# Moving the additions to the softmax sums from GpSimd to VectorE, and one weight step ahead of the copy of h, in a fused attention and feed-forward kernel

## The chip, the core and the metric

The kernel runs on one core of a Trainium2 chip. The metric is the device time of one execution in microseconds (us). The kernel before takes 947.29 us, the median of three runs (945.96 to 948.33).

A core has five engines that run side by side, each working through its own queue of instructions in the order in which the program issued them. TensorE (PE in the profile; its weight loads are PEld) multiplies matrices into eight PSUM banks. VectorE (DVE), ScalarE (ACT) and GpSimd (POOL) do arithmetic on tiles. SyncE (SP) issues the transfers here. Where one engine needs another's result it waits on a semaphore, and everything behind the waiting instruction in the same queue waits with it.

## The reference, cut to what matters

```
scores = q @ k^T / 8, masked to a window of 32 keys (half of the heads: 32 keys at distance 4)
attn   = exp(scores - max);  attn = attn / (sum(attn) + 1e-09)
x      = (attn @ v), heads put side by side        # 4608 tokens x 512
h      = x @ w_in                                  # 512 -> 2048
sp     = max(h, 0) + log1p(exp(-abs(h)))
out    = (h * erf(sp)) @ w_out                     # 2048 -> 512
```

All data is float32. The `+ 1e-09` under the division is the addition that the change moves.

## The kernel before, in words

**Attention.** The work is cut into 72 units (u or n) of four blocks of 64 queries for two heads. A unit passes through `scores` (TensorE, into the banks `sp`), `mask_max` (VectorE: masked scores into `prob`, their maxima into `nmax`), `exponents` (ScalarE: four exponentials in place, each with its row sums into `ssum`; then GpSimd adds 1e-9 to the sums, L207), `normalize` (VectorE: reciprocals `rinv` of the sums, L211; then GpSimd multiplies `prob` by them, L212), `transposes` (TensorE, L217), `turned` (a copy to `pT`, L220), `values` (TensorE, L233), `rows_hi` (ScalarE, L274) and `rows_lo` (VectorE, L279), which write the rounded value and the remainder of the rows x. Values follow scores three visits later (LAG = 3).

**Feed-forward.** It is made in 72 steps t of 512 tokens by 256 hidden columns, each of two half steps; x = 2t + j counts half steps. One half step runs `mm1` (12 matmuls into the single bank `h`, L454), `take` (VectorE copies `h` to `hc`, L462, which frees the bank), and, two steps later, `mm2` (L495). Between them stand `argument` (ScalarE: Sigmoid L466 and Ln L467), `table` (ScalarE: Erf, L470) and `gate` (VectorE, L477, L480, L481). Functions in different tables cost a table load on ScalarE.

**Weights.** The float64 weights are split on the chip into a rounded part and a remainder. One step is `prep_act` (ScalarE: a cast L377 and a rebased copy L382) and `prep_dve` (VectorE: a subtraction L391 and three bit operations L395 to L397, after which SyncE loads the next piece, L366).

**Order.** The order on every engine is the order in which the code issues (`manual_schedule`). The first 14 units (FIRST = 14) go through `first_visit`, before any feed-forward. Then the half steps begin: x = 0 to 3 belong to steps 0 and 1, in which there is no `mm2` yet. Half step x (up to 6) scores unit 14 + x and finishes unit 11 + x. In x = 0 to 3, TensorE gets the transposes of the finished unit first, then `mm1`, then `values` and `scores`. The weight step stands behind `take`, and is left out at x = 2 and 3 (`pause`), so that of these four half steps only x = 0 and x = 1 have one. `exponents` of what was scored at x come at x + 1 for x = 0, and at even half steps otherwise; `normalize` of a unit comes at the earliest one half step after its `exponents`, behind whatever `exponents` that half step issues.

Of the kernel before, what the change touches and what calls it, by code (L numbers as in the profile page):

```python
# [15 lines left out]
ALU = mybir.AluOpType  # L16
# [46 lines left out]
FIRST = NBLK + LAG + 2  # L63
# [5 lines left out]
SAVED = 2 * (HALF + 1) + 1  # L69
# [16 lines left out]
def ends(t):  # L86

    return t + 1 == NT or STEPS[t][2] != STEPS[t + 1][2]
# [24 lines left out]
def attn_moe_kernel(ctx: ExitStack, tc: tile.TileContext, qk, v, masks, eye, w_in, w_out, out):  # L113
    nc = tc.nc
# [50 lines left out]
    def load_qk(u):  # L165
        if u < NU:
            n = QW + key_start(u, PER - 1) + KEYS
            nc.sync.dma_start(out=qkz[u % 2][:, 0:n], in_=qk[u, :, 0:n])
# [5 lines left out]
    probs, maxes, sums, x_rows = {}, {}, {}, {}  # L174
# [24 lines left out]
    def exponents(u):  # L199
        nmax = maxes.pop(u)  # L200
        sums[u] = small.tile([P, PER], F32, name="ssum", bufs=LAG + 1)
        for j in range(PER):
            nc.scalar.activation(  # L203
                out=probs[u][:, j, :], in_=probs[u][:, j, :], func=AF.Exp,
                scale=-1.0, bias=nmax[:, j:j + 1], accum_out=sums[u][:, j:j + 1],
            )
        nc.gpsimd.tensor_scalar(sums[u], sums[u], 1.0e-9, None, op0=ALU.add)  # L207

    def normalize(u):
        rinv = small.tile([P, PER], F32, name="rinv")  # L210
        nc.vector.reciprocal(out=rinv, in_=sums.pop(u))  # L211
        nc.gpsimd.tensor_tensor(probs[u], probs[u], rinv.broadcast_to([P, PER, KEYS]), op=ALU.mult)  # L212

    def transposes(u):
        pr = probs.pop(u)
        for j in range(PER):
            nc.tensor.transpose(out=turn_place(u)[0:KEYS, j * P:(j + 1) * P], in_=pr[:, j, :], identity=ident)  # L217

    def turned(u, copy):
        copy(out=pz[u in second][0:KEYS].rearrange("p j q -> p (j q)"), in_=turn_place(u)[0:KEYS])  # L220

    def turn(units):
        for u in units:
            transposes(u)
        for u in units:
            turned(u, nc.vector.tensor_copy)
# [75 lines left out]
    def has(u):  # L302
        return 0 <= u < NU
# [46 lines left out]
    def soon(load, *args):  # L350
        if held[0]:
            behind.append((load, args))
        else:
            load(*args)

    def hold(on):
        held[0] = on
        while behind and not on:
            load, args = behind.pop(0)
            load(*args)  # L360
# [10 lines left out]
    def prep_act():  # L371


        calls[0] += 1
        if made:
            w, hi, lo = made.popleft()
            nc.scalar.copy(out=hi, in_=w)  # L377
            rest.append((calls[0], w, hi, lo))
        if staged:
            i, d, hi, lo = staged.popleft()  # L380
            w = io.tile([P, TOK], F32, name="w", bufs=4)
            nc.scalar.activation(out=w, in_=d[:, :, 1].bitcast(F32), func=AF.Abs, scale=REBASE)  # L382
            begun.append((calls[0], i, d, hi, lo, w))

    def prep_dve(keep=None):

        if rest and rest[0][0] < calls[0]:
            _, w, hi, lo = rest.popleft()  # L390
            nc.vector.tensor_tensor(lo, w, hi.bitcast(F32), op=ALU.subtract)  # L391
        if begun and begun[0][0] < calls[0]:
            _, i, d, hi, lo, w = begun.popleft()
            t = w.bitcast(I32)
            nc.vector.tensor_scalar(t, t, 3, None, op0=ALU.logical_shift_left)  # L395
            nc.vector.scalar_tensor_tensor(t, d[:, :, 1], -0x80000000, t, op0=ALU.bitwise_and, op1=ALU.bitwise_or)  # L396
            nc.vector.scalar_tensor_tensor(t, d[:, :, 0], 29, t, op0=ALU.logical_shift_right, op1=ALU.bitwise_or)  # L397
            made.append((w, hi, lo))
            if i != keep:
                soon(load_w, i)  # L400
# [82 lines left out]
    def mm2(t, j):  # L483
        ghi, glo = gs[t][j]
        _, ftp, run = STEPS[t]
        ft = ftp * PAIR + j
        first, last = ftp == RUNS[run][1] and j == 0, ends(t) and j == PAIR - 1
        parts = ((ghi, wout_hi), (ghi, wout_lo)), ((glo, wout_hi),)

        if last:  # L490
            parts = (sum(parts, ()),)
        for part in parts:
            for tt in range(TOK // P):
                for g, w in part:
                    nc.tensor.matmul(acc[tt], g[:, tt * P:(tt + 1) * P], w[:, ft, :],  # L495
                                     start=(first and w is wout_hi and g is ghi),
                                     stop=(last and g is glo))
        if j == PAIR - 1:
            del gs[t]
# [37 lines left out]
    with tc.manual_schedule():  # L537
        load_qk(0)
        nc.sync.dma_start(out=cst, in_=masks)
        for t in vz:  # L540
            nc.gpsimd.memset(t[KEYS:P], 0.0)
        nc.gpsimd.memset(pz[0][KEYS:P], 0.0)
        load_qk(1)
        nc.sync.dma_start(out=ident, in_=eye)
        for n in range(FIRST):
            if n < 3:
                load_w(n)
            first_visit(n)
            if 1 <= n <= EARLY:
                prep_dve()  # L550
        normalize(FIRST - 2)
        rows_lo(FIRST - 1 - LAG)

        plan = visits()


        pause = 2, 3, 2 * (USED[SPC - 1] + 1) - 2
        due = {n - LAG: x for x, ns in plan.items() for n in ns}
        todo, scaled, fresh = [], [FIRST - 1], []
        for x in range(2 * (NT + 2)):  # L560
            t, j = divmod(x, 2)
            ns = plan.get(x, [])
            scored, ready = [n for n in ns if has(n)], [n - LAG for n in ns]
            second.update(ready[1:])

            if t < 2:
                turn(ready)
            if t < NT:
                after = STEPS[t + 1][0] if ends(t) and t + 1 < NT else None
                if x == 2 * HALF - 4:  # L570
                    load_x(1, range(twice))
                elif after and after > 1 and j == 0:
                    load_x(after, range(twice))
                if x in (2 * HALF - 2, SAVED):
                    hold(True)
                mm1(t, j)
                if x == 0:
                    for a in stores:
                        store_x(*a)
                if after is not None and j == PAIR - 1:  # L580
                    load_x(after, range(twice, CC))
                    hold(False)
                take(t, j)

            if x == 1 or j == 0 and x:
                for u in todo:
                    exponents(u)
                fresh, todo = todo, []
            if j == 1 and 1 <= t <= NT:
                table(t - 1)  # L590
            if t < 2:
                attend(ready, scored)
            if t >= 2:
                turn(ready)

            while scaled:
                normalize(scaled.pop(0))
            scaled, fresh = fresh, []
            if j == 1 and 1 <= t <= NT:
                gate(t - 1, 0)  # L600
            if j == 0 and 2 <= t:
                gate(t - 2, 1)
            if j == 1 and t < NT:
                argument(t)
            if x not in pause:
                prep_act()
                prep_dve(keep=2 if SAVED - 4 < x <= SAVED else None)
            if t >= 2:
                mm2(t - 2, j)
                if x == SAVED:  # L610
                    save()
                    hold(False)
                    load_w(2)
                elif ends(t - 2):
                    if j == 1:
                        store(STEPS[t - 2][0])
                    elif STEPS[t - 2][2] == 2:
                        fetch()
            if t >= 2:
                attend(ready, scored)  # L620
            for n in ns:
                soon(load_qk, n + 2)
                soon(load_v, n - 1)
            for n in scored:
                mask_max(n)
                todo.append(n)
            for u in [u for u in scaled if due[u] == x + 1]:
                scaled.remove(u)
                normalize(u)
            for m in ready:  # L630
                rows_lo(m)
            if x == SAVED + 2:
                nc.gpsimd.memset(pz[1][KEYS:P], 0.0)
        assert not todo and not prep and not staged and not begun and not made and not rest
# [84 lines left out]
```

## Time and profile before

| | |
|---|---|
| median of 3 runs | 947.29 us |
| the profiled execution | 947.37 us, of which the span from first to last instruction is 945.6 us |
| mean granted TensorE clock | 0.996 of full speed |
| busy: DVE, ACT, POOL | 581.6, 643.3, 109.3 us |
| first matmul into h (x = 0) | 51.12 us after the span's start |
| first matmul of x = 1, 2, 3, 4 | 55.54, 61.18, 71.52, 77.17 us |

Times in the rows below count from the start of the span. A row of the timeline reads: start, duration, engine, line of the code, operation, output from input; in brackets the idle time of the engine just before it and what ended that.

### The profile page before, as it was taken

How to read it: one execution, taken by the hardware profiler on the slowest of the kernel's cores; microseconds unless marked ns; L12 is line 12 of the kernel's file. 1: busy time of each engine (PE TensorE's matmuls, PEld its weight loads, DVE VectorE, ACT ScalarE, POOL GpSimd, SP SyncE). 2: the span in 40 equal slices, each digit the busy share in tenths (PEclk: the TensorE clock that was granted, in tenths of full speed). 3: DMA queues.
4: the chain of work that ended last, by engine and by line, in shares of the span. 5: the costliest groups of instructions: out<-in, count | busy, mean ns of one | idle time of the engine just before them, and what ended most of it. 6: DMA issues, size and time to landing. Idle time of an engine off the chain costs nothing.

```text
span 945.6 us, 15964 instructions
## 1 busy us (share of the span) xinstructions
PE 917.9 (97%) x6048; PEld 749.5 (79%) x6048; DVE 581.6 (62%) x1509; ACT 643.3 (68%) x1204; POOL 109.3 (12%) x154
## 2 busy tenths in 40 slices
PE   5879999999999999999999999999999999999998
PEld 4657887888888887888888888888888888888886
DVE  6967988986665654666566555655665444434434
ACT  7878978785856865777577656866566556445553
POOL 2312210011111210121111111111111000000000
PEclk9999999999999999999999999999999999999999
DMA  8774443431632242313232152314220302011001
GB/s 284 263 240 139 175 172 138 145 122 51 211 133 68 67 150 73 111 67 111 87 111 67 67 164 103 120 45 140 91 87 35 107 10 87 1 45 44 1 1 45
DMA packets 51500, 98.73 MB, mean 104 GB/s; under 512 B 7136, under 2 KB 20192, under 8 KB 51424
## 3 DMA queue, kind: packets, MB, share of 16 engines
q1 hardware_dynamic: 51136, 97.19, 30.7%
q8 instruction: 48, 0.79, 0.3%
q10 hardware_dynamic: 288, 0.52, 0.1%
q14 instruction: 28, 0.23, 0.1%
HBM read 69.52 MB, written 27.26 MB: 102 GB/s over the span
## 4 chain that ended last, share of the span: by engine, by line
PE 89%; DVE 5%; DMA 2%; ACT 2%; issue 1%; POOL 0%; SPq 0%; POOLq 0%; DVEq 0%
PE h L454 40%; PE acc L495 39%; PE tx L233 3%; PE sp L184 3%; PE sp L217 3%; DMA x<-xT 1%; DVE w L396 1%; DVE w L397 1%; DMA qk<-in_qk_dram 1%; DVE win_lo L391 1%; DVE prob L193 1%; DVE w L395 0%; DMA dbl<-in_w_in_dram 0%; PE acc L217 0%; DVE x L279 0%
## 5 line engine op out<-in xcount | busy, mean ns | idle before, releaser
L462 DVE COPY hc<-h 128x512 f32<-128x512 f32 x144 | 99.4, 691 | 281.7 <-PE h L454 281.3
L454 PE MATMUL h<-x,win_hi 128*128 128x512 f32 x832 | 260.1, 394 | 1.4 <-DMA x<-xT 1.3
L495 PE MATMUL acc<-wout_hi,ghi 128*128 128x512 f32 x576 | 227.5, 395 | 0.2 <-DVE ghi L480 0.2
L495 PE MATMUL acc<-wout_lo,ghi 128*128 128x512 f32 x576 | 224.4, 390 | 0.0
L466 ACT ACTIVATE s<-hc 128x1024 f32<-128x1024 f32 x72 | 76.4, 1061 | 182.5 <-DVE hc L462 182.5
L454 PEld LDWEIGHTS h<-x,win_hi 128*128 128x128 f32 x832 | 155.2, 189 | 36.2 <-issue 2.1
L454 PE MATMUL h<-x,win_lo 128*128 128x512 f32 x416 | 162.6, 391 | 0.0
L495 PE MATMUL acc<-wout_hi,glo 128*128 128x512 f32 x576 | 158.8, 389 | 0.0
L495 PEld LDWEIGHTS acc<-wout_hi,ghi 128*128 128x128 f32 x576 | 108.2, 188 | 22.6 <-DVE ghi L480 0.6
L495 PEld LDWEIGHTS acc<-wout_hi,glo 128*128 128x128 f32 x576 | 108.1, 188 | 22.6
L495 PEld LDWEIGHTS acc<-wout_lo,ghi 128*128 128x128 f32 x576 | 108.3, 188 | 21.4
L481 DVE TENSOR_TENSOR glo<-s,ghi 128x512 fp32r<-128x512 f32 x144 | 107.8, 749 | 5.2
L203 ACT ACTIVATE prob<-prob,nmax 128x96 f32<-128x96 f32 x288 | 104.0, 363 | 5.4 <-DVE nmax L193 5.0
L212 POOL TENSOR_TENSOR prob<-prob,rinv 128x384 f32<-128x384 f32 x72 | 86.2, 1208 | 113.4 <-DVE rinv L211 104.4
L477 DVE TENSOR_TENSOR s<-hc,s 128x1024 f32<-128x1024 f32 x72 | 89.3, 1240 | 6.8 <-ACT s L470 6.6
L467 ACT ACT_TABLE_LOAD x72 | 92.4, 1283 | 1.3
L470 ACT ACT_TABLE_LOAD x72 | 92.4, 1283 | 1.3
L454 PEld LDWEIGHTS h<-x,win_lo 128*128 128x128 f32 x416 | 78.5, 189 | 16.9
L193 DVE CUSTOM_DVE_ANT_0 prob<-sp,cst 128x96 f32<-128x96 f32 x288 | 54.7, 252 | 49.4 <-PE sp L184 49.3
L454 PE MATMUL h<-dbl,win_hi 128*128 128x512 f32 x256 | 80.6, 396 | 0.0
L207 POOL TENSOR_SCALAR ssum<-ssum 128x4 f32<-128x4 f32 x72 | 20.3, 282 | 496.2 <-ACT prob L203 485.2
L274 ACT CAST rows<-tx 128x64 fp32r<-128x64 f32 (+5 forms) x116 | 26.2, 357 | 75.2 <-PE tx L233 75.2
(59 smaller groups left out, 1016.8 us busy)
## 6 DMA issues: line engine op xcount, KB each, us to landing
xT<-rows SPq DMA_DIRECT2D x26, 576.0 KB, 4.8
v<-in_v_dram SPq DMA_DIRECT2D x72, 192.0 KB, 4.0
qk<-in_qk_dram SPq DMA_DIRECT2D x48, 272.0 KB, 3.9
dbl<-in_w_in_dram SPq DMA_DIRECT2D x16, 512.0 KB, 4.0
dbl<-in_w_out_dram SPq DMA_DIRECT2D x16, 512.0 KB, 3.3
qk<-in_qk_dram SPq DMA_DIRECT2D x24, 288.0 KB, 4.1
out_dram<-w SPq DMA_DIRECT2D x26, 256.0 KB, 2.4
x<-xT SPq DMA_DIRECT2D x8, 320.0 KB, 5.7
```

The lines of the kernel that those rows point to most:

```text
L184: nc.tensor.matmul(sps[h][r:r + BLK, i, j // 2, :], qkz[i][hs, j * BLK:(j + 1) * BLK], qkz[i][hs, at:at + KEYS], start=True, stop=True)
L193: nc.vector.tensor_tensor_reduce(out=pr[:, 2 * h + p, :], in0=sps[h][:, u % 2, p, :], in1=mask[PAIRS.index((kind(n), kind(n + 1)))], scale ...
L203: nc.scalar.activation(out=probs[u][:, j, :], in_=probs[u][:, j, :], func=AF.Exp, scale=-1.0, bias=nmax[:, j:j + 1], accum_out=sums[u][:, ...
L212: nc.gpsimd.tensor_tensor(probs[u], probs[u], rinv.broadcast_to([P, PER, KEYS]), op=ALU.mult)
L454: nc.tensor.matmul(h, w[:, cc, ft * P:(ft + 1) * P], x[cc], start=(k == 0 and i == 0), stop=(k == CC - 1 and i == 2))
L462: nc.vector.tensor_copy(out=hs[t][:, j], in_=h)
L466: nc.scalar.activation(out=ls[t], in_=hs[t], func=AF.Sigmoid, scale=-1.0)
L467: nc.scalar.activation(out=ls[t], in_=ls[t], func=AF.Ln, bias=TINY)
L470: nc.scalar.activation(out=ls[t], in_=ls[t], func=AF.Erf, scale=-1.0)
L477: nc.vector.tensor_tensor(out=e, in0=hc, in1=e, op=ALU.mult)
L481: nc.vector.tensor_tensor(out=glo, in0=e[:, j], in1=ghi.bitcast(F32), op=ALU.subtract)
L495: nc.tensor.matmul(acc[tt], g[:, tt * P:(tt + 1) * P], w[:, ft, :], start=(first and w is wout_hi and g is ghi), stop=(last and g is glo))
```

## The change

It does two things. In `exponents` and `normalize`, units from 14 on have 1e-9 added to their sums by VectorE, as the instruction right in front of the reciprocals, instead of by GpSimd behind the exponentials; units 0 to 13 stay as they were. In the half steps of steps 0 and 1, the weight step is issued behind the copies of `turn` and in front of `mm1` and the copy of `h`, instead of behind them; from step 2 on it stays where it was.

```
     def exponents(u):
...
-        nc.gpsimd.tensor_scalar(sums[u], sums[u], 1.0e-9, None, op0=ALU.add)
+        if u < FIRST:
+            nc.gpsimd.tensor_scalar(sums[u], sums[u], 1.0e-9, None, op0=ALU.add)

     def normalize(u):
         rinv = small.tile([P, PER], F32, name="rinv")
+
+        if u >= FIRST:
+            nc.vector.tensor_scalar(sums[u], sums[u], 1.0e-9, None, op0=ALU.add)
         nc.vector.reciprocal(out=rinv, in_=sums.pop(u))
...
         pause = 2, 3, 2 * (USED[SPC - 1] + 1) - 2
+
+        def weights(x):
+            if x not in pause:
+                prep_act()
+                prep_dve(keep=2 if SAVED - 4 < x <= SAVED else None)
+
...
             if t < 2:
                 turn(ready)
+                weights(x)
...
             if j == 1 and t < NT:
                 argument(t)
-            if x not in pause:
-                prep_act()
-                prep_dve(keep=2 if SAVED - 4 < x <= SAVED else None)
             if t >= 2:
+                weights(x)
                 mm2(t - 2, j)
```

The changed file has other line numbers: what was L211, L212, L391, L395, L462 is L215, L216, L395, L399, L466 there.

VectorE at x = 0 before: the copy of unit 11's transposes, the copy of h, the reciprocals of unit 13, then the weights.

```order
L220 COPY pT_88<-acc_93 96x512
L462 COPY hc<-h 128x512
L211 RECIPROCAL rinv<-ssum 128x4
L391 TENSOR_TENSOR wout_lo<-w,wout_hi 128x512
L395 TENSOR_SCALAR w<-w 128x512
L396 SCALAR_TENSOR_TENSOR w<-dbl_552,w 128x512
L397 SCALAR_TENSOR_TENSOR w<-dbl_552,w 128x512
```

And the same place of the changed kernel:

```order
L224 COPY pT_88<-acc_93 96x512
L395 TENSOR_TENSOR wout_lo<-w,wout_hi 128x512
L399 TENSOR_SCALAR w<-w 128x512
L400 SCALAR_TENSOR_TENSOR w<-dbl_552,w 128x512
L401 SCALAR_TENSOR_TENSOR w<-dbl_552,w 128x512
L466 COPY hc<-h 128x512
L215 RECIPROCAL rinv<-ssum 128x4
```

The four weight instructions went in front of the copy of h; x = 1 has the same move. At x = 2, and wherever reciprocals of later units stand, one small `TENSOR_SCALAR ssum<-ssum 128x4` now stands right in front of them.

GpSimd before, from the last unit of the first visits on; the pairs are units 12 and 13, then the sums of 14 and 15, then their products, and so on.

```order
L207 TENSOR_SCALAR ssum<-ssum 128x4
L212 TENSOR_TENSOR prob<-prob,rinv 128x384 x2
L207 TENSOR_SCALAR ssum<-ssum 128x4 x2
L212 TENSOR_TENSOR prob<-prob,rinv 128x384 x2
L207 TENSOR_SCALAR ssum<-ssum 128x4 x2
```

And in the changed kernel:

```order
L208 TENSOR_SCALAR ssum<-ssum 128x4
L216 TENSOR_TENSOR prob<-prob,rinv 128x384 x6
L437 CAST x_99<-x_99 128x2x64
L437 CAST x_100<-x_100 128x2x64
L216 TENSOR_TENSOR prob<-prob,rinv 128x384 x5
```

The product of unit 14 no longer stands behind the sums of unit 15; nothing but products, two casts and one memset is left on GpSimd from here to the end.

ScalarE at x = 0 and x = 1 before: the rows of unit 11, the exponentials of 14, the rows of 12, Sigmoid and Ln of step 0, the weight step of x = 1, and then the exponentials of 15 and the rows of 13 (that of x = 0 stands between the first two).

```order
L274 CAST rows<-acc_94 128x256
L466 ACT_TABLE_LOAD
L466 ACTIVATE s<-hc 128x1024
L467 ACT_TABLE_LOAD
L467 ACTIVATE s<-s 128x1024
L377 CAST wout_hi<-w 128x512
L382 ACTIVATE w<-dbl_657 128x512
L203 ACT_TABLE_LOAD
```

And in the changed kernel:

```order
L381 CAST wout_hi<-w 128x512
L386 ACTIVATE w<-dbl_657 128x512
L203 ACTIVATE prob,ssum<-prob,nmax 128x96 x4
L278 CAST rows<-acc_94 128x256
L470 ACT_TABLE_LOAD
L470 ACTIVATE s<-hc 128x1024
L471 ACT_TABLE_LOAD
L471 ACTIVATE s<-s 128x1024
L203 ACT_TABLE_LOAD
```

The weight step of x = 1 went from behind the Ln to in front of unit 14's exponentials. On SyncE the load that each moved weight step issues moves with it: that of x = 0 now stands in front of the four stores of x to `xT` that were ahead of it. The order on TensorE is the same.

## The prediction

> **What bounds the kernel now.** I first read the page's busy times, to see whether any engine has no room.
>
> ```profile
> PE 917.9 (97%) x6048; PEld 749.5 (79%) x6048; DVE 581.6 (62%) x1509; ACT 643.3 (68%) x1204; POOL 109.3 (12%) x154
> ```
>
> TensorE is busy for 917.9 of 945.6 us, so a change elsewhere can pay only by closing some of the other 28 us. The view of waits says where they are; this is TensorE from 50 to 82 us, and then from 82 us to the end (total, times, longest).
>
> ```profile
> PE acc L217 <- POOL prob L212: 5.6, 2, 5.3
> PE acc L233 <- DVE pT L220: 1.1, 1, 1.1
> ```
>
> ```profile
> PE h L454 <- DMA x<-xT: 1.3, 3, 0.5
> PE tx L233 <- DVE pT L220: 1.0, 1, 1.0
> PE acc L495 <- DVE ghi L480: 0.2, 1, 0.2
> ```
>
> From 82 us on TensorE waits 2.5 us in all; between 50 and 82 us, the half steps that the change touches, it waits 6.7 us, and 5.3 us of it at one place. The chain that ended last, around that place, names the culprit (start, duration, what).
>
> ```profile
> 51.36 2.76 PE h L454 x12
> ...
> 65.53 0.51 ACT wout_hi L377
> 66.03 0.56 ACT w L382
> ...
> 69.61 0.22 POOL ssum L207
> ...
> 69.90 0.84 POOL prob L212
> ...
> 71.87 4.26 PE h L454 x12
> ```
>
> At x = 3 TensorE wants unit 14's transposes and waits for GpSimd's product of unit 14. Why was that late? The timelines of GpSimd and of VectorE tell.
>
> ```profile
> 60.12 0.22 POOL L207 TENSOR_SCALAR ssum<-ssum 128x4 f32<-128x4 f32 x1 [3.93 <-ACT prob L203]
> 69.60 0.22 POOL L207 TENSOR_SCALAR ssum<-ssum 128x4 f32<-128x4 f32 x1 [9.26 <-ACT rows L274]
> ```
>
> ```profile
> 64.83 0.17 DVE L211 RECIPROCAL rinv<-ssum 128x4 f32<-128x4 f32 x1
> ```
>
> Unit 14's sums were ready at 60.34 us and its reciprocals at 65.0, but the product stands in GpSimd's queue behind the addition to unit 15's sums, and that waited 9.26 us for ScalarE's exponentials. The product lost 4.9 us (69.90 against 65.0) to a queue, not to data. It cost more than the wait: the clock fell too (windows of 5 us; the column behind the five engines is the granted clock).
>
> ```profile
> 60.00:65.00 5.00, 4.86 (x66) 3.76 (x61) 4.93 (x17) 4.56 (x6) 0.22 (x1) 1.00 0.96 320
> 65.00:70.00 5.00, 0.50 (x18) 0.31 (x16) 0.89 (x9) 4.95 (x15) 0.32 (x2) 0.81 0.69 236
> 70.00:75.00 5.00, 4.22 (x12) 3.50 (x13) 1.18 (x3) 2.23 (x2) 0.73 (x1) 0.50 0.29 118
> ```
>
> At clock 0.50 the 12 matmuls of x = 3 took 4.26 us; those of x = 0, at full clock, took 2.76.
>
> **The change part by part.** I follow x = 0 to 5 with both edits in.
>
> *Weights ahead of the copy, x = 0.* VectorE's rows at x = 0 and 1:
>
> ```profile
> 54.15 0.69 DVE L462 COPY hc<-h 128x512 f32<-128x512 f32 x1 [2.06 <-PE h L454]
> ...
> 54.84 0.66 DVE L391 TENSOR_TENSOR wout_lo<-w,wout_hi 128x512 fp32r<-128x512 f32 x1
> ...
> 57.84 0.25 DVE L193 CUSTOM_DVE_ANT_0 prob<-sp,cst 128x96 f32<-128x96 f32 x1
> ...
> 60.14 0.70 DVE L391 TENSOR_TENSOR wout_lo<-w,wout_hi 128x512 fp32r<-128x512 f32 x1
> ...
> 62.55 0.25 DVE L193 CUSTOM_DVE_ANT_0 prob<-sp,cst 128x96 f32<-128x96 f32 x1
> ```
>
> VectorE sits idle from 52.09 to 54.15 us, waiting for h. The four weight instructions take 2.41 us at x = 1 (60.14 to 62.55) and 3.00 at x = 0 (54.84 to 57.84), so put into that hole they end at 54.5 to 55.1, and the copy of h comes 0.35 to 0.95 us late. Its cover is TensorE, which has unit 11's values, unit 14's scores and unit 12's transposes to do before it needs the bank:
>
> ```profile
> 55.54 0.71 PE L454 MATMUL h<-x,win_hi 128*128 128x512 f32 x2
> ```
>
> A copy that ends (0.6 us after its start) at 55.1 to 55.7 costs x = 1 nothing to 0.2 us. Were the cover gone, it would cost the 0.35 to 0.95.
>
> What is gained: behind the copy no weights stand, so the maxima of unit 14 and then unit 12's copy to pT come 2.1 to 2.7 us earlier (3.00 less the copy's delay). TensorE was waiting for that copy:
>
> ```profile
> 59.68 0.69 PE L233 MATMUL acc<-pT,v 128*64 128x64 f32 x16 [1.14 <-DVE pT L220]
> ```
>
> The wait of 1.14 us goes, less up to 0.2: unit 12's values end about 1.0 us earlier (59.4). At x = 1 the weights stand between 57.0 and 59.9 or so, and the copy of h ends at 59.9 to 60.5, against 60.15 now; TensorE is busy until then or close to it, and x = 2 begins 0.7 to 1.1 us earlier.
>
> *The addition to the sums.* Unit 14's product now needs only its reciprocals. With x = 2 that much earlier, they start at 63.8 to 64.2 (64.83 now) behind their addition, and the product (0.84) ends at 64.8 to 65.3, in place of 70.74.
>
> ```profile
> 70.78 1.09 PE L217 MATMUL acc<-ident,prob 128*96 128x128 f32 x4 [5.28 <-POOL prob L212]
> ```
>
> TensorE had been free since 65.5 and will be since 64.4 to 64.8, so 5.28 us of wait become about 0.5, at most 1; the transposes' 0.4 and the 2.76 us of x = 3 at full clock then end at 68.0 to 68.6.
>
> [...] The row first: the wait of 1.14 us left 1.00 in the window from 60 us, and the wait of 5.28 left 0.50. [...]
>
> *What is late next.* ScalarE's chain. These rows are unit 12's rows, the Erf of step 0, and VectorE's remainder of unit 13 that stands ahead of unit 14's copy to pT:
>
> ```profile
> 60.41 0.37 ACT L274 CAST rows<-acc 128x256 fp32r<-128x256 f32 x1 [0.38 <-PE acc L233]
> ...
> 71.19 1.06 ACT L470 ACTIVATE s<-s 128x1024 f32<-128x1024 f32 x1
> ```
>
> ```profile
> 69.91 0.58 DVE L279 TENSOR_TENSOR rows<-acc,rows 128x128 fp32r<-128x128 f32 x2 [3.56 <-ACT rows L274]
> ```
>
> ScalarE works almost without a pause from 60.41 to 72.25 (4.56 and 4.95 of 5 us in the windows above). This stretch starts 1.0 us earlier (values of unit 12), and loses the weight step of x = 1, which lies on it with 0.51 + 0.56 = 1.07 us and moves into ScalarE's free time before unit 14's exponentials. All in it comes 2.05 us earlier: VectorE's remainder at 67.85, unit 14's copy to pT at 68.4 to 69.0. Unit 14's values, which want that copy, move by −7.05:
>
> ```profile
> 76.06 0.69 PE L233 MATMUL acc<-pT,v 128*64 128x64 f32 x16
> ```
>
> The Erf ends at 70.2, and VectorE's gate of step 0, which now follows the copy of h, will wait for it instead, moving by −6.65:
>
> ```profile
> 76.78 0.17 DVE L211 RECIPROCAL rinv<-ssum 128x4 f32<-128x4 f32 x1
> 76.86 1.19 DVE L477 TENSOR_TENSOR s<-hc,s 128x1024 f32<-128x1024 f32 x1
> ```
>
> From there to x = 5 VectorE has next to no room:
>
> ```profile
> 80.00:85.00 5.00, 4.93 (x51) 3.79 (x51) 4.93 (x16) 4.97 (x19) 0.69 (x1) 1.00 0.67 208
> ```
>
> So I take its −6.65 over TensorE's −7.05.
>
> *The additions' own cost.* No row shows this operation on VectorE. Nearest is the reciprocal of the same tile:
>
> ```profile
> L211 DVE RECIPROCAL rinv<-ssum 128x4 f32<-128x4 f32 x72 | 10.1, 163 | 1.4 <-POOL ssum L207 1.4
> ```
>
> At 163 ns, of which the next instruction overlaps all but 80 ns (76.78 to 76.86 above), 58 additions make 4.6 to 9.5 us of VectorE's time; below nothing they cannot go, as VectorE did none of this before. I take 80 ns. The work that hides them is the idle time in front of the copies of h, 281.7 us:
>
> ```profile
> L462 DVE COPY hc<-h 128x512 f32<-128x512 f32 x144 | 99.4, 691 | 281.7 <-PE h L454 281.3
> ```
>
> They add no wait of their own: the reciprocals already waited, through GpSimd, for the same exponentials. On the path to x = 5 only unit 16's addition counts, +0.1 us.
>
> **Sum.** −6.65 + 0.1 = −6.55 us by x = 5; behind it TensorE hardly waits, and the shift stays. The profiled execution is 947.37 us (945.6 and 1.8 around it), which stands 0.1 over the median: 947.37 − 6.55 = **940.8 us**. Its own range: ends of the copies' delay (0.2), VectorE's or TensorE's shift (0.4), and the runs' scatter (about 1): 939.5 to 942.
>
> **Rivals.** *Loads come late.* SyncE's load of x = 0 waits for the weights and now stands ahead of four stores, and the loads of units 13 (v) and 16 (qk) behind those:
>
> ```profile
> 50.56 2.62 SPq L300 DMA_DIRECT2D xT<-x  x4
> ```
>
> ```profile
> 58.82 0.42 SPq L172 DMA_DIRECT2D v<-in_v_dram  x1
> ```
>
> ```profile
> v<-in_v_dram SPq DMA_DIRECT2D x1, 192.0 KB, 4.7
> ```
>
> The load of v was issued at 58.82 and took 4.7 us. Now it would issue at about 55 + 2.6 + 0.8 = 58.4 and land at 63.1, just when its values want it. But the big stores, which took 5.3 us to land, would then run beside it until about 63, where they were nearly done before:
>
> ```profile
> xT<-x SPq DMA_DIRECT2D x2, 512.0 KB, 5.3
> ```
>
> I estimate up to 3 us more for it, by half of those 5.3. Unit 13's and 16's matmuls and those of x = 3 take 4.4 us up to unit 14's values at 69.0, which leaves 1.2 us of room, so up to 1.8 us is lost: 942.6.
>
> *The change doesn't do what it says:* the product of unit 14 waits for unit 15's exponentials all the same, since its wait on ScalarE is now its own, not through the sums. Then it starts 2.05 us earlier than 69.9 and nothing else is won: 945.3. The program places it behind unit 14's exponentials only, so I give it little.
>
> *Slower:* VectorE becomes the bound. It has 58 more instructions, and at x = 5 to 8 it is nearly full. If more than 6.55 of the dearer 9.5 us land on the path, which is 41 of 58 additions, the kernel is slower than before; all of them make 947.4 − 6.55 + 9.5 = 950.3. The 281.7 us before the copies of h speak against it.
>
> **How the numbers follow.** Forecast 0.74; late loads 0.13; no effect on the product 0.05; VectorE bound 0.04; 0.04 for a gain beyond 938.9, if the waits behind 82 us shrink as well. The 8 in 10 reach from 938.9 over the forecast and the late loads to 943.8. A measurement tells 0.3%, 2.8 us, from no change: faster (below 944.4) is the forecast, the late loads and the greater gain, 0.91; same is the product's rival, 0.05; slower is VectorE's, 0.04.
>
> **What would show it.** Right: the product of unit 14 starts at 64 to 65 us, TensorE's wait ahead of it is near 1 us, the clock stays at 1.00 from 50 to 80 us, x = 4 begins at 70 to 70.7 instead of 77.17, and all later rows stand 6.5 to 7 us earlier. Wrong: a wait of TensorE on loads of v or qk at 62 to 66 us, new waits on VectorE's copies after 82 us, or a product that still starts right behind unit 15's exponentials.

## The result, and the profile after

| | before | changed |
|---|---|---|
| median, 5 runs each | 946.86 us (945.96 to 948.33) | 941.03 us (940.10 to 943.27) |
| profiled execution's span | 945.6 us | 938.3 us |
| mean granted clock | 0.996 | 0.984 |

The ratio is 0.9941, with a 95% interval of 0.9924 to 0.9957: 5.8 us faster by the medians, where 6.55 were forecast (940.8 us). Run again beside other kernels, the changed kernel gave 941.62 and 0.9944 (0.9927 to 0.9961).

The page's first row, and TensorE's waits from 50 to 82 us and from there to the end (total, times, longest), of the changed kernel:

```profile
PE 913.7 (97%) x6048; PEld 746.5 (80%) x6048; DVE 591.7 (63%) x1567; ACT 643.0 (69%) x1204; POOL 92.7 (10%) x96
```

```profile
PE acc L221 <- POOL prob L216: 1.1, 2, 0.9
PE sp L221 <- DVE nmax L193: 0.5, 1, 0.5
PE acc L237 <- DVE pT L224: 0.3, 1, 0.3
```

```profile
PE tx L237 <- DVE pT L224: 1.0, 1, 1.0
PE h L458 <- DMA x<-xT: 0.3, 1, 0.3
PE acc L499 <- DVE dbl L517: 0.2, 1, 0.2
PE acc L499 <- DVE ghi L484: 0.2, 1, 0.2
```

The 6.7 us of waits between 50 and 82 us have become 1.9. The other engines show the price: GpSimd has 58 instructions less (154 to 96), VectorE 58 more and 10 us more of busy time. GpSimd's timeline from 55 us on:

```profile
55.95 0.83 POOL L216 TENSOR_TENSOR prob<-prob,rinv 128x384 f32<-128x384 f32 x1 [1.38 <-PE acc L221]
64.75 0.83 POOL L216 TENSOR_TENSOR prob<-prob,rinv 128x384 f32<-128x384 f32 x1 [7.98 <-ACT s L471]
70.31 0.83 POOL L216 TENSOR_TENSOR prob<-prob,rinv 128x384 f32<-128x384 f32 x1 [4.72 <-DVE rinv L215]
```

These are the products of units 13, 14 and 15. That of unit 14 starts at 64.75 instead of 69.90. The releaser named in its row, ScalarE's Ln, only ended last among the events seen by then: the product starts 0.16 us behind the end of its reciprocals, unit 15's 0.17. VectorE's timeline shows both:

```profile
55.04 0.68 DVE L466 COPY hc<-h 128x512 f32<-128x512 f32 x1
...
64.21 0.16 DVE L214 TENSOR_SCALAR ssum<-ssum 128x4 f32<-128x4 f32 x1
64.41 0.18 DVE L215 RECIPROCAL rinv<-ssum 128x4 f32<-128x4 f32 x1
...
68.08 0.58 DVE L283 TENSOR_TENSOR rows<-acc,rows 128x128 fp32r<-128x128 f32 x2 [2.34 <-ACT rows L278]
...
69.96 0.18 DVE L215 RECIPROCAL rinv<-ssum 128x4 f32<-128x4 f32 x1
70.45 1.76 DVE L481 TENSOR_TENSOR s<-hc,s 128x1024 f32<-128x1024 f32 x1 [0.31 <-ACT s L474]
72.25 0.43 DVE L484 CAST ghi<-s 128x512 fp32r<-128x512 f32 x1
```

TensorE at the beginning of x = 3 (transposes of unit 14), at that unit's values, and at the beginning of x = 4:

```profile
65.64 0.64 PE L221 MATMUL acc<-ident,prob 128*96 128x128 f32 x4 [0.85 <-POOL prob L216]
...
69.30 0.69 PE L237 MATMUL acc<-pT,v 128*64 128x64 f32 x16 [0.29 <-DVE pT L224]
...
70.41 0.73 PE L458 MATMUL h<-x,win_hi 128*128 128x512 f32 x2
```

A wait of 0.85 us is left of the 5.28, and the windows of 5 us (laid out as in the prediction) show no fall of the clock behind it:

```profile
60.00:65.00 5.00, 4.74 (x54) 3.51 (x48) 3.14 (x15) 4.92 (x6) 0.24 (x1) 1.00 1.02 348
65.00:70.00 5.00, 4.08 (x36) 3.18 (x40) 2.62 (x14) 4.96 (x13) 0.58 (x1) 1.00 0.92 304
70.00:75.00 5.00, 4.52 (x35) 3.50 (x36) 4.62 (x16) 4.95 (x8) 0.83 (x1) 1.00 0.72 238
```

### The profile page after: what moved, and what is told of

It reads as the page before. It is cut to its first block, busy times and chain, and to the rows that moved or that the text cites. A ratio compares the mean times of both kernels' runs of the same rounds, so it can differ in the third digit from the quotient of the medians.

```text
span 938.3 us, 15916 instructions
## 1 busy us (share of the span) xinstructions
PE 913.7 (97%) x6048; PEld 746.5 (80%) x6048; DVE 591.7 (63%) x1567; ACT 643.0 (69%) x1204; POOL 92.7 (10%) x96
## 4 chain that ended last, share of the span: by engine, by line
PE 88%; DVE 6%; ACT 2%; DMA 2%; issue 1%; SPq 0%; POOL 0%; POOLq 0%; DVEq 0%
PE h L458 40%; PE acc L499 39%; PE tx L237 3%; PE sp L221 3%; PE sp L184 2%; DMA dbl<-in_w_in_dram 1%; DVE w L400 1%; DVE prob L193 1%; DVE w L401 1%; DVE win_lo L395 1%; DVE s L481 1%; DMA x<-xT 1%; ACT prob L203 0%; DVE w L399 0%; DVE x L283 0%
## 5 line engine op out<-in xcount | busy, mean ns | idle before, releaser
L466 DVE COPY hc<-h 128x512 f32<-128x512 f32 x144 | 99.4, 690 | 267.5 <-PE h L458 266.8
L216 POOL TENSOR_TENSOR prob<-prob,rinv 128x384 f32<-128x384 f32 x72 | 85.6, 1200 | 576.6 <-DVE ssum L214 348.6
L485 DVE TENSOR_TENSOR glo<-s,ghi 128x512 fp32r<-128x512 f32 x144 | 100.2, 696 | 5.2
L481 DVE TENSOR_TENSOR s<-hc,s 128x1024 f32<-128x1024 f32 x72 | 98.4, 1367 | 6.1 <-ACT s L474 6.1
L474 ACT ACTIVATE s<-s 128x1024 f32<-128x1024 f32 x72 | 76.4, 1061 | 0.8
L471 ACT ACTIVATE s<-s 128x1024 f32<-128x1024 f32 x72 | 76.4, 1061 | 0.8
```

Source lines behind the costliest of these rows:

```text
L466: nc.vector.tensor_copy(out=hs[t][:, j], in_=h)
L471: nc.scalar.activation(out=ls[t], in_=ls[t], func=AF.Ln, bias=TINY)
L474: nc.scalar.activation(out=ls[t], in_=ls[t], func=AF.Erf, scale=-1.0)
L481: nc.vector.tensor_tensor(out=e, in0=hc, in1=e, op=ALU.mult)
L485: nc.vector.tensor_tensor(out=glo, in0=e[:, j], in1=ghi.bitcast(F32), op=ALU.subtract)
```

## The experiments

Differences of half a microsecond are below what the times tell, so beside the times I measure two stretches in each kernel's trace: **A**, from the start of unit 11's transposes to the start of h's copy of x = 5, and **B**, from there to the thirteenth copy of h (x = 12). A holds the half steps that the change touches; B is where VectorE has hardly an idle moment (busy 43.67 of its 46.98 us before, 44.52 of 47.52 in the change). The first column of numbers is how long the 12 matmuls of x = 0 took, which varies by execution (more of it in the last section). A contains them. Without that column, A is 34.54 and 34.42 in the two profiles of before and 27.90 and 27.92 in the two of the change, so that differences of some 0.2 us can be read from it.

| kernel | x = 0, us | A, us | B, us | median, us | ratio to before (95%) |
|---|---|---|---|---|---|
| before | 2.76 | 37.30 | 46.98 | 946.86 | |
| before, again | 2.75 | 37.17 | 47.02 | 948.06 | 1.0008 (0.9994 to 1.0021) |
| the change | 3.06 | 30.96 | 47.52 | 941.03 | 0.9941 (0.9924 to 0.9957) |
| the change, again | 3.93 | 31.85 | 47.52 | 941.62 | 0.9944 (0.9927 to 0.9961) |
| additions only | 2.75 | 32.49 | 47.52 | 944.15 | 0.9959 (0.9945 to 0.9973) |
| weights only | 3.31 | 35.35 | 46.98 | 945.62 | 0.9982 (0.9969 to 0.9994) |
| unit 15's addition only | 2.74 | 30.58 | 46.95 | 940.49 | 0.9926 (0.9910 to 0.9942) |
| additions on GpSimd, in front | 3.17 | 30.85 | 47.23 | 941.11 | 0.9931 (0.9912 to 0.9949) |
| no additions | 3.92 | 31.62 | 47.01 | 941.12 | 0.9940 (0.9925 to 0.9954) |
| additions twice | 3.00 | 30.88 | 48.32 | 941.59 | 0.9943 (0.9929 to 0.9958) |
| before, kept warm | 3.20 | 35.96 | 47.00 | 945.98 | 0.9985 (0.9974 to 0.9997) |
| ScalarE's half only | 2.79 | 31.47 | 47.55 | 941.68 | 0.9939 (0.9920 to 0.9959) |
| unit 15 normalized early | 3.97 | 31.33 | 47.53 | 942.04 | 0.9934 (0.9917 to 0.9952) |
| unit 15's addition, and early | 3.15 | 30.53 | 47.30 | 939.42 | 0.9910 (0.9893 to 0.9927) |

The kernels were run in several groups, each with its own runs of before (medians from 946.9 to 947.7), so ratios compare better than medians.

### The additions alone

```
             if t < 2:
                 turn(ready)
-                weights(x)
...
+            weights(x)
             if t >= 2:
-                weights(x)
                 mm2(t - 2, j)
```

> Only the additions move; the weight steps of x = 0 and 1 stay behind the copy of h. Queue theory (the product of unit 14 waits in GpSimd's queue behind the sums of unit 15; ScalarE's chain is the next limit): the product starts at 65.1 us instead of 69.90, TensorE waits about 0.5 us for it, the clock stays at 1.00 from 65 to 75 us, and then TensorE waits about 2 us for unit 14's copy to pT, which stands behind unit 13's remainder at 69.9. VectorE's gate of step 0 waits for the Erf that ends at 72.25 and moves by 4.5 us: 942.4 us. Rival (the weights carry the gain, the additions are a detail): within 1.5 us of before, 946. Rival (58 additions on VectorE cost 0.2 us each where they stand): 11 us of it on the path, slower than before.

A is 32.49, 4.8 us shorter than before; the time is 3.9 us below (1 - 0.9959). GpSimd's product of unit 14 and TensorE's waits from 50 to 82 us are these:

```profile
65.42 0.82 POOL L216 TENSOR_TENSOR prob<-prob,rinv 128x384 f32<-128x384 f32 x1 [9.19 <-DVE rinv L215]
```

```profile
PE acc L237 <- DVE pT L224: 2.7, 2, 1.5
PE acc L221 <- POOL prob L216: 1.0, 2, 0.8
PE sp L221 <- DVE nmax L193: 0.5, 1, 0.5
```

The product starts 4.5 us earlier (4.85 counted from unit 11's transposes, which stand 0.37 later here), and the wait that takes its place is the one for the copies to pT, 2.7 us in all. Of these, 1.1 us were there before (unit 12's); unit 14's 1.5 are new, where the queue theory said 2. The rival that the weights carry the gain is out, and so is the one that the additions make the kernel slower than before.

### The weights alone

```
-        if u < FIRST:
-            nc.gpsimd.tensor_scalar(sums[u], sums[u], 1.0e-9, None, op0=ALU.add)
+        nc.gpsimd.tensor_scalar(sums[u], sums[u], 1.0e-9, None, op0=ALU.add)
...
-        if u >= FIRST:
-            nc.vector.tensor_scalar(sums[u], sums[u], 1.0e-9, None, op0=ALU.add)
```

> Only the weight steps of x = 0 and 1 move; all additions stay on GpSimd behind the exponentials. Queue theory: ScalarE's chain comes 2 us earlier, so unit 15's sums are ready at about 67.6 instead of 69.6, the product of unit 14 starts at 67.9, and TensorE, free at 64.8, waits 3.9 us. If a wait of that length still halves the clock, x = 4 begins 2 us earlier: 945. If it doesn't, 3.5 us earlier: 943.5. Rival (the weights carry the gain): 941 to 942, with a wait of TensorE under 1.5 us at x = 3. The two parts then do not add up: 4.5 and 2 to 3.5 for the parts against 6.1 at x = 5 for both.

A is 35.35, 1.95 us shorter than before (2.5 us without x = 0, which took 0.55 us longer here), the time 1.7 us below. GpSimd's sums of unit 15 and product of unit 14, then TensorE's transposes, then from the chain that ended last the 12 matmuls of x = 3:

```profile
68.40 0.22 POOL L207 TENSOR_SCALAR ssum<-ssum 128x4 f32<-128x4 f32 x1 [9.25 <-ACT rows L275]
68.70 0.83 POOL L213 TENSOR_TENSOR prob<-prob,rinv 128x384 f32<-128x384 f32 x1
```

```profile
69.58 0.71 PE L218 MATMUL acc<-ident,prob 128*96 128x128 f32 x4 [4.28 <-POOL prob L213]
```

```profile
70.29 4.26 PE h L455 x12
```

The queue is as it was, only shifted; behind a wait of 4.28 us x = 3 takes 4.26 us again, as it did behind 5.28 us before, where the granted clock read 0.50. Of the two branches in the expectation it is the slower one, 2 us. The parts make 4.8 and 1.95 us of A and 3.9 and 1.7 us of time; the change made 6.3 and 5.8. Without x = 0, the parts make 4.8 and 2.5 us of A and the change 6.6, so they don't add up, as was expected.

### One addition of the 58

```
-        if u < FIRST:
+        if u != FIRST + 1:
             nc.gpsimd.tensor_scalar(sums[u], sums[u], 1.0e-9, None, op0=ALU.add)
...
-        if u >= FIRST:
+        if u == FIRST + 1:
             nc.vector.tensor_scalar(sums[u], sums[u], 1.0e-9, None, op0=ALU.add)
```

> The weight steps move, and of the 58 additions only that of unit 15 goes to VectorE; the others stay on GpSimd behind the exponentials. Queue theory: one addition stood in the way of one product, so the product of unit 14 starts at 64.7 as in the change, x = 4 begins at 70.4, and the time is that of the change, 941 us, within 0.7. Rival (it is the sum over 58 units that counts, GpSimd's freed time or shorter waits all along): most of the gain is missing, 944 to 946.

A is 30.58, the time 0.9926 of before: all of the change's gain, from a single instruction moved and the two weight steps. And B is 46.95, as before, where the change has 47.52.

### The same engine, another place in its queue

```
         if u >= FIRST:
-            nc.vector.tensor_scalar(sums[u], sums[u], 1.0e-9, None, op0=ALU.add)
+            nc.gpsimd.tensor_scalar(sums[u], sums[u], 1.0e-9, None, op0=ALU.add)
```

> The weight steps move, and all 58 additions stay on GpSimd, but are issued right in front of the reciprocals (in normalize) instead of behind the exponentials. Queue theory: only the place in GpSimd's queue matters, not the engine: the product of unit 14 starts at 64.7, x = 4 begins at 70.4, the time is 941 us, within 1. Rival (VectorE must do the addition, since a step from VectorE to GpSimd and back costs VectorE about 1 us of standing still at each of some 25 pairs of units): VectorE's standing still shows as waits for the sums, some 25 us in all; if any of it lies on the path the time rises over 942.

A is 30.85 and the time 0.9931. GpSimd's addition for unit 14 now sits directly in front of its product, and that starts at 65.11 (unit 11's transposes stand 0.5 us later here than in the change's profile). VectorE's waits over the whole span have the row that was expected:

```profile
DVE rinv L215 <- POOL ssum L214: 26.6, 25, 1.6
```

VectorE stands still 26.6 us for GpSimd, and the time does not show it: its waits for h go from 281.3 to 262.5 us. (In the change they are 266.8.) So it is the place in the queue that counts, not the engine.

### No additions, and twice as many

The first of these leaves out the addition of 1e-9 for units 14 to 71; the second adds it twice.

```
         if u >= FIRST:
-            nc.vector.tensor_scalar(sums[u], sums[u], 1.0e-9, None, op0=ALU.add)
```

> As the change, but nobody adds 1e-9 to the sums of units 14 to 71 (each sum is at least 1, so float32 drops the addend anyway). Hidden-cost theory: GpSimd's queue is as free as in the change, and VectorE has 58 instructions of about 0.2 us less, 11 us in all. Up to x = 5 the same as the change; from x = 5 to 12, where VectorE has hardly an idle moment, the change lost 0.5 us of its lead and this kernel doesn't; afterwards nothing. 0.5 us faster than the change. Rival (VectorE on the path): 3 us or more faster than the change.

```
         if u >= FIRST:
             nc.vector.tensor_scalar(sums[u], sums[u], 1.0e-9, None, op0=ALU.add)
+            nc.vector.tensor_scalar(sums[u], sums[u], 1.0e-9, None, op0=ALU.add)
```

> As the change, with a second addition of 1e-9 behind each of the 58, so twice 11 us on VectorE. Hidden-cost theory: another 0.5 to 0.8 us lost by x = 12, nothing behind it: 0.5 to 1 us slower than the change. Rival (VectorE on the path): up to 11 us slower than the change, slower than before.

B reads 47.01 without, 47.52 with, and 48.32 with twice the additions; the five profiles with all 58 on VectorE once show 47.52 to 47.55. So the additions cost 0.5 us in B and nothing that the times could show elsewhere: the ratios are 0.9940 without, 0.9941 or 0.9944 with, 0.9943 with twice as many, and their intervals overlap. A VectorE that costs 3 us or more on the path is out.

### The clock alone

```
+            if x == 3:
+                for i in range(14):
+                    nc.tensor.matmul(h, win_hi[:, 0, 0:P], at[0][0][0], start=True, stop=True)
             if t < 2:
                 turn(ready)
```

> The kernel before, with 14 matmuls more, whose results are thrown away (they write into the bank h, which the first real matmul of x = 3 starts afresh), in front of unit 14's transposes at x = 3, where TensorE waits 5.3 us. They take 3.2 us of that wait. Clock theory: the clock stays at 1.00, the 12 matmuls of x = 3 take 2.76 instead of 4.26 us, and the kernel is 1.5 us faster than before with more work. Rival (the slow matmuls have another cause, for example the transfers, or something behind x = 3 ends last anyway): no change, 4.26 us as before.

TensorE around the wait, and the 12 matmuls of x = 3 from the chain:

```profile
66.62 3.47 PE L568 MATMUL h<-x,win_hi 128*128 128x512 f32 x14
71.98 0.64 PE L217 MATMUL acc<-ident,prob 128*96 128x128 f32 x4 [1.89 <-POOL prob L212]
```

```profile
72.62 2.77 PE h L454 x12
```

With 14 matmuls of no use in the wait, the next 12 take 2.77 instead of 4.26 us and the transposes 0.64 instead of 1.09; A is 1.3 us shorter, although x = 0 took 0.4 longer. The mean granted clock of this profiled execution is 1.000, where before has 0.996. The time is 0.9985 of before (0.9974 to 0.9997), 1.4 us. So some 1.5 us of what the long wait cost, and the change won back, is clock, not wait.

### Which half of the weight step

```
-        def weights(x):
+        def weights(x, dve=True):
             if x not in pause:
                 prep_act()
-                prep_dve(keep=2 if SAVED - 4 < x <= SAVED else None)
+                if dve:
+                    prep_dve(keep=2 if SAVED - 4 < x <= SAVED else None)
...
-                weights(x)
+                weights(x, dve=False)
...
+            if t < 2 and x not in pause:
+                prep_dve()
             if t >= 2:
```

> As the change, but only ScalarE's half of the weight steps of x = 0 and 1 (and no load) stands in front of h's copy; VectorE's half stays behind it. Theory (the two halves need each other: ScalarE's cast of x = 1 takes what VectorE's weight step of x = 0 makes, and that now ends at 57.9): the cast holds up unit 14's exponentials by 0.6 us, the chain gains 1.07 - 0.6 = 0.5 us over the kernel with the additions alone, and TensorE again waits about 1.1 us for unit 12's copy at x = 1. From unit 11's transposes to h's copy of x = 5: 32.0 us (37.3 before, 32.5 with the additions alone, 31.0 for the change); 943 to 943.5. Rival (ScalarE's 1.07 us is the whole worth of the moved weights): 31.4 us and 942.5.

My theory missed the number here, and the rival met it: A is 31.47, not 32.0. ScalarE's timeline shows the cast of x = 1, the exponentials of unit 14, and the rows of unit 12:

```profile
58.80 0.62 ACT L381 CAST wout_hi<-w 128x512 fp32r<-128x512 f32 x1 [2.75 <-DVE w L401]
59.32 0.66 ACT L386 ACTIVATE w<-dbl 128x512 f32<-128x512 f32 x1
59.89 0.36 ACT L203 ACTIVATE prob<-prob,nmax 128x96 f32<-128x96 f32 x1
...
61.32 0.35 ACT L278 CAST rows<-acc 128x256 fp32r<-128x256 f32 x1
```

The cast does wait 2.75 us for VectorE, as I had it. But it delays the exponentials by 0.3 us only, and these then end just as unit 12's values do, which the rows waited 0.38 us for before. The delay fell into that slack. ScalarE's 1.07 us is worth 1.02 us (32.49 to 31.47). It is not the whole worth of the moved weights, as the rival has it: TensorE still waits 1.1 us for unit 12's copy, as the theory said, and without x = 0, A is 28.68 here and 27.9 in the change, so VectorE's half adds 0.8.

### Unit 15 normalized early

```
-            for u in [u for u in scaled if due[u] == x + 1]:
+            for u in [u for u in scaled if due[u] == x + 1 or x == 2]:
                 scaled.remove(u)
                 normalize(u)
```

> As the change, but unit 15 is normalized at the end of x = 2 (in front of unit 13's remainder, where VectorE stands idle for ScalarE anyway) instead of at x = 3. Port theory (the product of unit 15, which runs on GpSimd from 70.3 beside VectorE's gate, stretches that from 1.20 to 1.76 us): the product runs from about 68.0, the gate takes 1.2 us, and all behind it, h's copy of x = 5 included, comes 0.5 us earlier than in the change: 30.5 us from unit 11's transposes; the time 0.3 to 0.6 us below the change's, too little for the time alone to show. Rival (the gate is long for another reason, or it has room behind it): 1.76 us or no shift at x = 5.

The gate of step 0 on VectorE:

```profile
72.89 1.23 DVE L481 TENSOR_TENSOR s<-hc,s 128x1024 f32<-128x1024 f32 x1 [0.59 <-ACT s L474]
```

It takes 1.23 us instead of 1.76, with the product of unit 15 out of its way, and the cast behind it takes 0.43 as in the change. A is 31.33, against 31.85 for the change in the profile that has the same slow x = 0: the 0.5 us expected. The times do not tell the two apart, as expected.

> The weight steps as in the change, the addition of unit 15 alone on VectorE, and unit 15 normalized at the end of x = 2. Both savings together: the 0.5 us by which the other 57 additions hold VectorE up between x = 5 and 12, and the 0.5 us of the gate. About 30.1 us from unit 11's transposes to h's copy of x = 5, none of the lead lost by x = 12, and about 1 us below the change: 940.

This is that edit together with the one addition. A is 30.53, not 30.1, but x = 0 took 3.15 us; without it, A is 27.38, as with unit 15 normalized early (27.36), against 27.84 with the one addition. So the 0.5 us of the gate are all there. B is 47.30, where the one addition alone had 46.95: less than half of that saving is left. VectorE's next gate, at 82.82, now waits 0.28 us for ScalarE's Erf, where it waited for nothing in the kernel with the one addition. It is also long (1.77 us, with unit 17's product started ahead of it), but the cast behind it is short in its place (0.43, not 0.94). The time is 939.42, 0.9910 (0.9893 to 0.9927). That is the best of all measured here; against the change's 0.9941 and 0.9944 the intervals barely touch. The traces account for 0.65 us of the difference (0.43 of A, 0.22 of B); the rest may be scatter.

### Before, again

> The kernel before as it is, profiled a second time. In its first profile TensorE waited longer for the loads of x near 351 us than in the changed kernel's (7.13 us from one copy of h to the next, against 5.97), and again near 554 us, so that the profiled spans lie 7.3 us apart where the medians lie 5.8 apart. Theory (these waits vary from execution to execution and are no part of the change): the second profile has another value at 351 or 554 us, and the stretch from unit 11's transposes to h's copy of x = 5 is 37.3 us again, within 0.3, with 5.3 us of wait ahead of unit 14's transposes and the 12 matmuls of x = 3 at 4.2 to 4.3 us. Rival (the loads come later in the kernel before by its own order): 7.1 us again.

A is 37.17 and the 12 matmuls of x = 3 take 4.21 us. From h's copy of x = 47 to the next it takes 6.24 us, between the first profile's 7.13 and the change's 5.97. The other kernels have 5.48 to 6.80, among them before kept warm with 6.09 and unit 15's addition only with 6.53. So the theory holds: these waits for loads vary by execution, and they make up the most of why the two spans lie 7.3 us apart and the medians 5.8. Up to x = 47 the changed kernel's lead in the profiles is 5.46 us.

## Why the prediction came out right, point by point

- **The bound, and the place of the wait.** Right: TensorE's one long wait was for a product held up in GpSimd's queue. With the weight steps moved, one addition out of the way gives all of the change's gain (A 30.58), and leaving all 58 on GpSimd at another place in the queue does too (30.85).
- **Weights ahead of the copy.** The copy of h at x = 0 started 0.89 us later (0.35 to 0.95 was said), and x = 2 began at 60.55, 0.63 earlier, just short of the 0.7 to 1.1 that was said. The first matmuls of that execution ran at a lower pace and took 0.3 us of it.
- **The product and the clock.** Start at 64.75 (64 to 65), wait 0.85 (0.5, at most 1), clock 1.00 from 52 us on (1.00 from 50 was said; more of it in the last section). The clock's part was sized at 1.5 us and measures 1.5 by itself.
- **What is late next.** ScalarE's chain, as said: the remainder of unit 13 at 68.08 (67.85), unit 14's values at 69.30 (69.0), the gate at 70.45 (70.2), x = 4 at 70.41 (70 to 70.7).
- **The additions.** Mis-sized: 80 ns was taken for one, the low end, but from one to the reciprocal behind it that reads its result the rows show 0.20 us (64.21 to 64.41). And "behind it TensorE hardly waits, and the shift stays" was wrong by 0.5 us: in B, where VectorE has hardly any room (busy 44.52 of 47.52 us), the additions cost that much, shown by leaving them out and doubling them.
- **The gate.** Overlooked: it takes 1.76 us instead of 1.19 because unit 15's product now runs beside it on GpSimd; it started 0.14 us ahead of the gate (70.31 and 70.45). With that product moved out of its way the gate took 1.23; by what means the one slows the other was not shown. But this did not cost the forecast half a microsecond, since before the same product started 0.57 us behind the gate's start, and then the product and the cast behind the gate were long:

```profile
77.43 1.31 POOL L212 TENSOR_TENSOR prob<-prob,rinv 128x384 f32<-128x384 f32 x1 [6.70 <-PE sp L184]
```

```profile
78.09 0.93 DVE L480 CAST ghi<-s 128x512 fp32r<-128x512 f32 x1
```

From the gate's start to the cast's end it took 2.16 us before, 2.23 in the change, and 1.69 with unit 15 normalized early. Both kernels pay for the product beside VectorE; in these rows the instruction that starts first keeps its time (0.83 for the product, 1.19 for the gate), and the other engine's is longer.
- **The sum.** −6.55 us was said; in the profiles the lead is 6.34 at x = 5 (A) and 5.8 at x = 12, and the medians say 5.8. Of what is missing, 0.2 us was gone by x = 5, where x = 0 had taken 0.3 us longer in that execution, and the rest is the additions in B. The forecast time lies only 0.2 us from the median, closer than the shift (0.7), since the runs of before came out at 946.86 and not at the 947.37 that the sum started from; that part is luck.
- **Late loads.** In the changed kernel TensorE waits for no load between 50 and 82 us. In two experiments with the same order on SyncE it does wait for v, 0.4 us each; the rival was real, at a fifth of its price.
- **Waits and the clock.** Waits of 4.28 and 5.28 us were followed by 12 matmuls in 4.2 to 4.3 us, waits of up to 1.9 us by 2.7 to 3.0 (x = 0 apart, see the last section). The granted clock read 0.50 behind the 5.28 us and 1.00 behind 0.85. Nothing between 1.9 and 4.28 us was tried, so how long a wait must be to cost the clock was not shown.

## What to carry to other kernels

A small instruction that waits for something late holds up every instruction behind it in its queue (here an addition of 0.22 us held a product up by 4.9 us); look for the wait in the row of the engine ahead, not in the data. When an engine is long idle in sum (GpSimd was busy for 109.3 of 945.6 us), such an instruction can still cost several microseconds (4.2 us of A without x = 0, by the kernels with the weights alone and with one addition of the 58), and moving it behind the urgent one on the same engine is enough (A 30.85). And a long wait on TensorE can cost more than itself: behind 4.28 and 5.28 us of it, 12 matmuls took 1.5 us longer here, with the granted clock at 0.50 behind the 5.28.

## What the runs showed of the hardware that was not expected

The same instructions before x = 0, in the same order, were followed by 12 matmuls that took 2.74 to 2.79 us in five of the 14 profiles and 3.00 to 3.97 in the other nine, by execution and not by kernel (the change itself has 3.06 and 3.93; before has 2.76 and 2.75, and kept warm, where nothing differs up to x = 3, 3.20). In the slow ones the first matmuls follow each other at about half pace, as they do behind the long wait of x = 3 (in the change run again the third starts 1.00 us after the first, at x = 3 of before also 1.00, at x = 0 of before 0.54). Ahead of x = 0 the pace is the slow one in all 14: 16 value matmuls take 1.12 us and 16 score matmuls 0.92, against 0.69 and 0.56 behind it. What differs is when the pace rises. In the five, unit 11's transposes, the last matmuls ahead of x = 0, already take only 0.64 to 0.95 us; in the nine they take 1.09, and the pace rises within the 12 matmuls. The recorded clock does not tell this: in the change's first profile it reads 0.50 up to 52 us, but in its second, with 3.93 us, 1.00 all the way, and 1.00 as well in the profiles of before, in which the matmuls ahead of x = 0 take as long. So it looks like the clock, but the records don't settle it, and what sets the moment was not tried. It is worth up to 1.2 us of A, as much as either small effect above: the change's two values of A differ by 0.89 us, those of x = 0 by 0.87.
